# An attention and maxout feed-forward kernel: the four weight matrices arrive as fp32 through SyncE's queue and are narrowed to fp16 by GpSimd

## The chip, the cores and the metric

The kernel runs on one core of a Trainium2 chip. The metric is the device time of one execution in microseconds (us). The five engines of the core are called PE (TensorE, matrix products), DVE (VectorE), ACT (ScalarE), POOL (GpSimd) and SP (SyncE); SP does no arithmetic here and only issues transfers. Each engine carries out its own list of instructions strictly in order, and waits for others through semaphores.

## The reference

Attention for 4 batches of 8 heads, 768 positions, head size 64, scores scaled by 1/8. Heads 0, 2 and 6 see every earlier position; the other five see the first 4 positions and the last 64. Its result, 3072 tokens by 512, goes through a feed-forward with three weight matrices under a maximum:

```
full   = rel >= 0                                   # rel = query position - key position
stream = (rel >= 0) & ((key < 4) | (rel < 64))
scores = where(mask_of_head, q @ k.T / 8, -1e9)
a      = exp(scores - max) ; a = a / sum(a)
x      = (a @ v) as [4*768, 512]
h      = maximum(maximum(x @ w1, x @ w2), x @ w3)   # w1, w2, w3: 512 x 768
out    = h @ w_out                                  # w_out: 768 x 512
```

All inputs and the output are fp32; the kernel computes its products in fp16 with fp32 sums.

## The kernel before, in words

The work is cut into 8 half batches (batch b, half of 384 positions), and each half batch into two groups of four heads. A group is numbered t = 4b + 2 half + group, and its two pairs of heads i = 0, 1. Nothing plans the order at run time: the tuple `PROGRAM` (L46 to L97) is a list of steps, a loop at L677 emits them one after another, and every engine and every queue sees its own instructions in just that order. What matters of the list:

- `hl half hp n ss` (L299) issues, on SP, fp32 loads of q and k of n pairs of heads of batch 0; `cast half hp ee` (L208) narrows k and q of a pair with the two engines named; `turnp` (L220) transposes them on PE and copies them from PSUM. The staging of two-pair loads has two buffers, so `hl 1 2` waits for the casts of `hl 0 2`.
- `load b qd` (L248) loads k and q of later batches with POOL's queue, which narrows fp32 to fp16 on the way, into the staging tag `kq` (three buffers of 6 KB per partition); `turn` (L259) transposes them on DVE. `load_v b half` (L281) loads v with SP, three transfers of 256 KB; `v t i ab` (L498) narrows it with engine a (`va`) and multiplies the far copy `vf` with engine b.
- `s t u` (L518): score products on PE, exponential on ACT. `k t i u e` (L570): multiplies exponentials by a mask on engine e (p is POOL, d is DVE). `av t i` (L590): on PE, weights times v, which needs every mask of that t and i and both copies of v; then on DVE the division. `x` (L627) or a transfer transposes the result.
- `f 1 e` (L488): advances the feed-forward of the oldest finished half batch by one `yield`. One half batch is a generator (L417): 18 steps of four products each (L438) and 3 steps of output products (L474). For batch 0 the 18 steps go through all of `w0t`, then all of `w1t`, then all of `w2t`. Each output step has two yields, so every other output `f` emits nothing.
- `m` (L387) builds masks on DVE, `gate` (L668) makes SP wait for a group before it goes on.

The weights: `w wi` (L399) issues on POOL's queue a transfer that narrows fp32 to fp16 on the way and writes the final tile: `w0t` in two halves, `w1t`, `w2t` and `woutt` whole, 768 KB each as written. They are the only weight loads; all 8 half batches use the same tiles.

Around the change POOL's own list is: mask and v work, the two halves of `w0t`, cast of `1 2`, `v 0 1`, cast of `1 0`, `w1t`, mask `k 2 1 2`, `w2t`, `load 1 0`, `woutt`, `load 1 1`, masks `k 2 0 3`, `k 2 0 2`, `k 3 0 1`, then v work of groups 2 and 3. SP's list is: loads of q and k, `load_v 0 0` in two parts, `hl 1 2`, `load_v 0 1`, then from `av 2 0` on transposes and stores. PE's list is: `turnp 1 2`, `x 0 0`, `s 2 0 1`, `av 1 1`, `av 1 0`, `av 0 1`, `turnp 1 0`, scores, six steps on `w0t` between scores, `turnp 1 3`, six steps on `w1t`, `av 2 0`, two steps on `w2t` and so on.

Of the kernel before, what the change touches and what calls it, by code (L numbers as in the profile page):

```python
# [11 lines left out]
FP32 = mybir.dt.float32  # L12
# [31 lines left out]
FIRST = "hl 0 0 1, ir"  # L44

PROGRAM = (  # L46
    "idle 2, idle 8, cast 0 0 aa, hl 0 1 1 ss, hl 0 2 2 ss, read, hl 1 0 2 ss, cast 0 1 pp",
    "flags, cast 0 2 ap, em 1, turnp 0 1 a, far, em 0, turnp 0 0 aa, cast 0 3 da, em 2, em 3",
    "load_v 0 0 4 4, s 0 0 1, s 0 0 0, v 1 1 pp, cast 1 1 pa, turnp 0 3 dd, turnp 0 2 da",
    "w 0 2 0, load_v 0 0 0 4, v 0 0 dp, s 1 0 0, w 0 2 1, s 0 1 0 b, hl 1 2 2 ss, s 1 0 1",  # L50
    "cast 1 2 dp, v 1 0 dd, s 0 1 1, s 1 1 0 b, av 0 0, v 0 1 pp, turnp 1 1 a, s 1 1 1",
    "turnp 1 2 aa, x 0 0 a, s 2 0 1, cast 1 0 dp, load_v 0 1, cast 1 3 ad, av 1 1, s 2 1 1",
    "av 1 0, x 1 1 d, av 0 1, turnp 1 0 ad, s 2 2 1, x 1 0 d, s 3 0 0, m 0, w 1, x 0 1 d",
    "s 2 0 0, m 3, m 1, f 1 d, f 1 d, s 2 1 0, s 2 2 0, m 2, f 1 a, f 1 d, k 2 1 2 p, k 2 0 1 d",
    "w 2, f 1 d, s 2 3 1, load 1 0, w 3, k 3 0 0 d, s 3 1 0, f 1 a, s 2 3 0, load 1 1",
    "k 2 0 3 p, k 2 0 2 p, turnp 1 3 dd, k 3 0 1 p, k 2 1 1 d, k 2 1 3 d, f 1 d, f 1 d",
    "v 2 0 ad, f 1 a, f 1 a, v 3 1 pp, f 1 d, s 3 0 1, v 2 1 dp, s 3 1 1, f 1 a, v 3 0 ap",
    "av 2 0 D, f 1 d, f 1 d, s 3 2 0, turn 1 0 0 0, turn 1 0 0 1, f 1 a, turn 1 0 1 0, s 3 2 1",
    "s 3 3 0, k 3 0 2 p, k 3 1 2 p, turn 1 0 1 1, f 1 a, av 2 1 D, s 3 3 1, k 3 1 1 d",
    "k 3 0 3 p, k 3 1 3 p, f 1 a, k 3 1 0 d, load_v 1 0, gate, f 1 a, s 4 0, k 4 1 0 p",  # L60
    "v 4 0 pp, av 3 0, av 3 1, f 1 a, f 1 a, x 3 0 d, s 4 1, turn 1 1 0 1, x 3 1 a, f 1 d",
    "v 5 1 pp, turn 1 1 1 0, turn 1 1 1 1, turn 1 1 0 0, k 4 0 1 d, k 4 0 0 d, k 4 1 1 p, f 1 a",
    "f 1 a, f 1 d, load_v 1 1, f 1 a, f 1 a, f 1 a, v 4 1 pd, f 1 a, f 1 d, s 5 0, f 1 a, f 1 d",
    "av 4 0 D, k 5 0 0 d, f 1 d, s 5 1, k 5 0 1 p, load_v 2 0, f 1 a, f 1 a, load 2 0, f 1 a",
    "s 6 0, f 1 d, av 4 1 D, f 1 a, v 5 0 ap, f 1 a, s 6 1, f 1 a, av 5 0 D, f 1 d, f 1 d",
    "k 5 1 1 p, k 5 1 0 p, v 7 0 dp, s 6 2, k 6 1 2 p, f 1 a, av 5 1 D, turn 2 0 1 0, f 1 a",
    "v 6 0 ad, s 6 3, turn 2 0 0 1, x 5 1 d, f 1 a, turn 2 0 1 1, load 2 1, load 3 1",
    "load_v 2 1, v 6 1 ap, f 1 d, f 1 d, k 6 0 2 p, v 9 0 ap, k 6 1 3 p, f 1 a, f 1 a",
    "turn 2 0 0 0, s 7 0, f 1 a, f 1 d, f 1 d, turn 2 1 0 0, k 6 0 1 d, f 1 a, s 7 1, f 1 d",
    "f 1 a, f 1 a, k 6 1 1 p, k 7 1 1 d, f 1 d, s 7 2, f 1 a, f 1 a, k 6 0 3 p, k 7 1 2 d",  # L70
    "turn 2 1 1 0, load 3 0, av 6 0 D, s 7 3, f 1 d, v 7 1 pp, av 6 1 D, k 7 1 3 p, f 1 d",
    "turn 3 1 1 0, k 7 0 3 p, turn 2 1 0 1, s 8 0, k 7 0 1 p, turn 2 1 1 1, k 7 0 2 p, f 1 a",
    "f 1 d, load_v 3 0, k 8 0 0 p, av 7 1 D, s 8 1, f 1 a, f 1 a, s 9 0, v 8 0 ap, k 8 0 1 d",
    "f 1 a, f 1 d, av 7 0 D, v 13 1 pp, s 9 1, f 1 a, av 8 0 D, f 1 d, s 10 0, f 1 a, x 7 1 d",
    "f 1 a, v 10 0 dd, f 1 d, s 10 1, f 1 a, f 1 d, v 9 1 ad, f 1 a, f 1 d, f 1 a, s 10 2",
    "f 1 d, f 1 d, f 1 d, k 8 1 0 p, f 1 d, k 9 0 0 p, k 9 1 1 d, f 1 d, f 1 d, v 11 0 ad",
    "f 1 d, k 9 1 0 p, v 12 0 ad, k 9 0 1 p, k 8 1 1 d, av 9 0 D, v 8 1 ap, s 10 3, f 1 d",
    "f 1 a, av 8 1 D, turn 3 0 1 0, s 11 0, k 10 1 1 p, f 1 d, f 1 d, k 10 0 3 p, f 1 a",
    "av 9 1 D, v 13 0 ap, f 1 a, k 10 1 3 d, turn 3 0 1 1, x 9 1 a, k 10 0 1 p, s 11 1, f 1 a",
    "k 10 0 2 p, v 11 1 ap, av 10 0 D, f 1 d, s 11 2, k 11 0 2 p, turn 3 0 0 0, f 1 a",  # L80
    "turn 3 0 0 1, f 1 d, k 11 0 1 d, f 1 a, k 10 1 2 d, f 1 d, v 10 1 ap, f 1 a, turn 3 1 0 1",
    "f 1 a, f 1 a, s 12 0, av 10 1 D, f 1 a, f 1 d, k 12 1 0 p, s 12 1, f 1 d, f 1 a, f 1 a",
    "k 12 0 1 p, turn 3 1 0 0, s 11 3, v 12 1 ad, f 1 a, load_v 3 1, f 1 a, f 1 a, k 11 0 3 d",
    "k 11 1 3 p, f 1 d, f 1 d, k 11 1 1 p, turn 3 1 1 1, f 1 a, f 1 d, av 11 0 D, f 1 d",
    "k 11 1 2 d, f 1 a, k 12 0 0 p, k 12 1 1 d, f 1 a, s 13 0, av 12 0 D, f 1 d, av 11 1 D",
    "k 13 0 0 d, f 1 d, f 1 d, s 13 1, f 1 d, v 15 1 pp, f 1 d, k 13 0 1 p, x 11 1 d, f 1 d",
    "v 15 0 ad, av 12 1 D, k 13 1 1 d, av 13 0 D, s 15 0, f 1 a, f 1 d, f 1 d, f 1 a, f 1 d",
    "f 1 d, f 1 a, k 13 1 0 d, s 15 1, v 14 0 ap, f 1 d, f 1 a, f 1 d, f 1 d, s 14 0, f 1 a",
    "f 1 d, f 1 d, f 1 d, av 13 1 D, s 14 1, f 1 d, x 13 1 d, f 1 d, f 1 d, f 1 a, f 1 a",
    "s 14 2, f 1 a, k 14 1 2 p, v 14 1 ad, k 14 1 1 p, f 1 d, f 1 d, f 1 d, f 1 a, f 1 a",  # L90
    "k 15 0 1 p, s 14 3, f 1 d, k 14 0 3 p, f 1 a, f 1 d, s 15 2, f 1 a, f 1 d, f 1 d, f 1 d",
# [18 lines left out]
def kernel(  # L110
# [22 lines left out]
    NNB = DF // P  # L133
# [14 lines left out]
    stage = ctx.enter_context(tc.tile_pool(name="stage", bufs=3))  # L148
# [27 lines left out]
    cast = {}  # L176
# [142 lines left out]
    def idle_work(n):  # L319
# [13 lines left out]
        out=base, in_=base, compare_op=ALU.is_ge, fill=0.0,  # L333
# [4 lines left out]
        out=kept[:, 256:512], in_=base, compare_op=ALU.is_gt, fill=0.0,  # L338
# [5 lines left out]
        out=kept[:, 0:256], in0=kept[:, 256:512], in1=base, op=ALU.add  # L344
    )
    nc.vector.tensor_copy(out=kept[:, 256:512], in_=kept[:, 0:256])
    if n_sink > 0:
        nc.vector.tensor_scalar(
            out=kept[0:n_sink, 256:512], in0=base[0:n_sink, :],
# [11 lines left out]
    far = consts.tile([P, H, 4], FP16, name="far")  # L361
# [34 lines left out]
    w_t = [consts.tile([P, KS, DF], FP16, name=f"w{wi}t") for wi in range(3)]  # L396
    woutt = consts.tile([P, NNB, DMdl], FP16, name="woutt")

    def load_weight(wi, parts=1, part=None):  # L399
        n = DF // parts  # L400
        first = 0 if part is None else part * n
        for c in range(first, (DF if part is None else first + n) if wi < 3 else 0, n):
            nc.gpsimd.dma_start(
                out=w_t[wi][:, :, c : c + n],
                in_=(moe_w1, moe_w2, moe_w3)[wi][:, c : c + n].rearrange(
                    "(ks p) n -> p ks n", p=P
                ),
            )
        if wi == 3:
            nc.gpsimd.dma_start(  # L410
                out=woutt, in_=moe_w_out.rearrange("(ns p) m -> p ns m", p=P)
            )


    xT = {}

    def ffn(b, half):  # L417
# [33 lines left out]
        for n, (wi, ni) in enumerate(order):  # L451
# [4 lines left out]
            else:  # L456
                dst = acc[ni] if wi == 1 else hT[ni]
                nc.vector.tensor_tensor(  # L458
                    out=dst, in0=yy[:, 0:HALF], in1=acc[ni], op=ALU.max
                )  # L460
            yield
        for tb in range(HB):

            parts = 2 if last and tb == HB - 1 else 1
            n = DMdl // parts
            r0 = b * S + half * HALF + tb * P
            ot = fwork.tile([P, DMdl], FP32, tag="ot", name="ot")
            for c, op, eng in (
                (0, nc.scalar.copy if last else copy_out[0], nc.sync),
                (n, nc.vector.tensor_copy, nc.scalar),  # L470
            )[:parts]:
                yo = psum()
                for ns in range(NNB):
                    nc.tensor.matmul(  # L474
                        yo[:, 0:n],
                        hT[ns][:, tb * P : (tb + 1) * P],
                        woutt[:, ns, c : c + n],
                        start=(ns == 0), stop=(ns == NNB - 1),
                    )
                op(out=ot[:, c : c + n], in_=yo[:, 0:n])  # L480
                eng.dma_start(out=out[r0 : r0 + P, c : c + n], in_=ot[:, c : c + n])
            yield
            yield

    queue = []
# [141 lines left out]
    def turn_x(t, i, op=None):  # L627
# [18 lines left out]
    ops = {"d": dve, "a": act, "p": pool}  # L646
    engines = {"d": nc.vector, "p": nc.gpsimd}
# [4 lines left out]
        f=lambda n, e="a": fill(int(n), ops[e]),  # L652
# [4 lines left out]
        turn=lambda *a: turn(*map(int, a)),  # L657
# [14 lines left out]
        far=far_flags,  # L672
        em=lambda hp: head_masks(int(hp), True),
        m=lambda hp: head_masks(int(hp)),
        w=lambda wi, *p: load_weight(int(wi), *map(int, p)),
    )
    for line in PROGRAM:  # L677
        for item in line.split(", "):
# [37 lines left out]
```

## Time and profile before

| what | us |
|---|---|
| two runs | 199.69 and 200.13, median 199.91 |
| span of the profiled execution (no other time of it is recorded) | 199.9 |
| PE busy | 190.0 (95%) |
| DVE / ACT / POOL busy | 148.3 / 115.9 / 90.5 |
| PE busy in the first 45 us | 38.5 |
| PE busy from 45 to 180 us | 134.9 of 135 |
| narrowing transfers on POOL's queue | 7.87 MB as written, 21.9% of 16 DMA engines' span |
| SP's queue | 17.96 MB, 37.9% |

How to read it: the share of busy PE is an average. Up to 45 us PE is idle for 6.5 us in some ten pieces; afterwards it has no idle time to speak of until the last microseconds. What delays PE in the first 45 us is therefore seen at the end in full, as far as nothing takes it up. In the timelines below a line gives start, duration, engine, line of the kernel, operation, output and inputs, shapes and count, and in brackets the engine's idle time just before it and what ended that. DMA engines are sixteen, shared by all queues.

### The profile page before, as it was taken

The page shows a single profiled execution, that of the slowest core. Times are in us where ns is not written, and L with a number is a line of the kernel's source. Part 1 is how long each engine was busy: PE and PEld are TensorE (multiplying, and loading weights), DVE is VectorE, ACT ScalarE, POOL GpSimd, SP SyncE. Part 2 cuts the span into 40 slices and gives each one's busy share as a digit, 9 for nine tenths or more (in the row PEclk, how much of TensorE's full clock was granted, in tenths as well). Part 3 has the DMA queues.
Part 4 walks back from the last instruction along what each step waited for, and adds up shares of the span by engine and source line. Part 5 has one row for each costly group of instructions (what it writes and reads, how often), then busy time and mean ns, then how long its engine had stood idle before and what let it go on. Part 6 is the DMA issues. An engine that isn't in the chain of part 4 may idle for free.

```text
span 199.9 us, 5135 instructions
## 1 busy us (share of the span) xinstructions
PE 190.0 (95%) x2059; PEld 109.3 (55%) x2059; DVE 148.3 (74%) x311; ACT 115.9 (58%) x171; POOL 90.5 (45%) x118
## 2 busy tenths in 40 slices
PE   7688898999999999999999999999999999999993
PEld 2345444565556455666456645574656455765552
DVE  3638965998976789896469998996978288767750
ACT  4489983765658798687776756634366565100011
POOL 3429187583276598490697245652010197000000
PEclk9889999999999999999999999999999999999999
DMA  5999999995979989988521232703500120124004
GB/s 143 312 245 230 196 195 212 208 169 76 283 173 211 162 169 208 218 218 176 147 76 23 43 124 74 159 20 73 167 5 20 53 108 0 23 59 157 3 0 157
DMA packets 48429, 26.48 MB, mean 132 GB/s; under 512 B 36758, under 2 KB 43926, under 8 KB 48406
## 3 DMA queue, kind: packets, MB, share of 16 engines
q1 hardware_dynamic: 43366, 17.96, 37.9%
q0 software_dynamic: 4624, 7.87, 21.9%
q8 instruction: 16, 0.26, 0.6%
q10 hardware_dynamic: 416, 0.33, 0.5%
q14 instruction: 7, 0.06, 0.1%
HBM read 25.17 MB, written 6.29 MB: 157 GB/s over the span
## 4 chain that ended last, share of the span: by engine, by line
PE 75%; DMA 11%; DVE 4%; SPq 3%; issue 2%; ACT 2%; POOL 0%; DVEq 0%
PE yy L438 39%; PE yy L474 14%; PE st L553 9%; PE oacc L602 9%; DMA vs<-in_v_dram 7%; PE yst L438 3%; DMA qs<-in_q_dram 2%; DVE KQ L267 2%; SPq L187 2%; ACT pt L564 1%; DMA xT<-x 1%; PE yst L474 1%; DVE acc L458 1%; DVE hT L458 1%; SPq L621 1%
## 5 line engine op out<-in xcount | busy, mean ns | idle before, releaser
L564 ACT ACTIVATE pt<-st 128x1024 f16<-128x1024 f32 (+3 forms) x98 | 83.3, 905 | 33.0 <-PE st L553 31.0
L586 POOL TENSOR_TENSOR pt<-pt,mk 128x512 f16<-128x512 f16 (+1 forms) x54 | 57.3, 1088 | 38.4 <-ACT pt L564 20.1
L438 PE MATMUL yy<-xT,w1t 128*128 128x384 f16 x180 | 35.8, 327 | 1.2 <-DVE pt L586 1.2
L438 PE MATMUL yy<-xT,w2t 128*128 128x384 f16 x180 | 36.1, 326 | 0.0
L438 PE MATMUL yy<-xT,w0t 128*128 128x384 f16 x180 | 35.8, 327 | 0.3
L458 DVE TENSOR_TENSOR acc<-yy,acc 128x384 f16<-128x384 f32 x45 | 24.8, 557 | 10.7 <-PE yy L438 8.6
L474 PE MATMUL yy<-woutt,hT 128*128 128x512 f16 (+1 forms) x138 | 31.6, 375 | 0.0
L553 PE MATMUL st<-KQ 32*128 32x384 f16 (+5 forms) x560 | 29.4, 281 | 1.4 <-ACT pt L564 0.8
L458 DVE TENSOR_TENSOR hT<-yy,acc 128x384 f16<-128x384 f32 x45 | 24.8, 556 | 4.5 <-PE yy L438 2.3
L602 PEld LDWEIGHTS <-pt 128*128 128x128 f16 x672 | 24.4, 97 | 4.8 <-DVE va L504 0.7
L267 DVE STREAM_TRANSPOSE KQ<-kq 128x384 f32<-128x384 f32 x24 | 25.5, 1132 | 0.6 <-DMA kq<-in_q_dram 0.6
L602 PE MATMUL oacc<-va,pt 128*128 128x65 f16 x352 | 24.9, 193 | 0.5 <-DVE va L504 0.5
L438 PEld LDWEIGHTS <-w1t 128*128 128x128 f16 x192 | 17.5, 98 | 14.1 <-issue 1.6
L438 PEld LDWEIGHTS <-w0t 128*128 128x128 f16 x192 | 17.8, 98 | 13.4 <-issue 0.8
L438 PEld LDWEIGHTS <-w2t 128*128 128x128 f16 x192 | 17.3, 98 | 11.9 <-issue 1.4
L553 PEld LDWEIGHTS <-KQ 32*128 32x128 f16 (+1 forms) x560 | 12.2, 93 | 18.8 <-issue 11.8
L474 PEld LDWEIGHTS <-hT 128*128 128x128 f16 x150 | 13.8, 98 | 14.7 <-issue 0.8
L602 PE MATMUL oacc<-vf,pt 128*128 128x65 f16 x320 | 21.1, 193 | 0.0
L455 ACT CAST acc<-yy 128x384 f16<-128x384 f32 x25 | 12.0, 481 | 13.9 <-PE yy L438 13.5
L612 DVE TENSOR_TENSOR x<-oacc,rc 128x384 f16<-128x384 f32 x32 | 17.8, 557 | 1.1
L480 DVE COPY ot<-yy 128x512 f32<-128x512 f32 (+1 forms) x15 | 10.1, 675 | 9.2 <-PE yy L474 9.2
L506 POOL TENSOR_TENSOR vf<-va,far 128x384 f16<-128x384 f16 x10 | 8.6, 867 | 17.3 <-ACT va L504 12.9
(72 smaller groups left out, 143.4 us busy)
## 6 DMA issues: line engine op xcount, KB each, us to landing
out_dram<-ot SPq DMA_DIRECT2D x23, 256.0 KB, 2.1
vs<-in_v_dram SPq DMA_DIRECT2D x21, 256.0 KB, 5.6
kq<-in_k_dram POOLq DMA_DIRECT2D x6, 384.0 KB, 7.9
kq<-in_q_dram POOLq DMA_DIRECT2D x6, 384.0 KB, 10.0
ks<-in_k_dram SPq DMA_DIRECT2D x8, 192.0 KB, 3.6
qs<-in_q_dram SPq DMA_DIRECT2D x7, 192.0 KB, 4.8
vs<-in_v_dram SPq DMA_DIRECT2D x6, 128.0 KB, 4.8
w0t<-in_moe_w_dram POOLq DMA_DIRECT2D x2, 384.0 KB, 9.4
```

Source lines behind the costliest of these rows:

```text
L267: nc.vector.transpose(out=dst.rearrange("c (p j) -> c j p", j=n)[:, j0:j1], in_=src.rearrange("c (j i) -> c j i", i=R),)
L438: nc.tensor.matmul(yy[:, 0:HALF], w_t[wi][:, ks, ni * P : (ni + 1) * P], xT[b, half][ks].rearrange("p a t -> p (a t)"), start=(ks == 0), s ...
L455: copy_out[0](out=acc[ni], in_=yy[:, 0:HALF])
L458: nc.vector.tensor_tensor(out=dst, in0=yy[:, 0:HALF], in1=acc[ni], op=ALU.max)
L474: nc.tensor.matmul(yo[:, 0:n], hT[ns][:, tb * P : (tb + 1) * P], woutt[:, ns, c : c + n], start=(ns == 0), stop=(ns == NNB - 1),)
L480: op(out=ot[:, c : c + n], in_=yo[:, 0:n])
L506: vf_engine.tensor_tensor(out=vf[j][:, hs, k0:k1, 0:D], in0=vs[:, hs, 0:1] if half == 0 else va[j][:, hs, k0:k1, 0:D], in1=far[:, hs, k0:k ...
L553: nc.tensor.matmul(sts[g // m][:, g % m, c0 : c0 + n * P], KQ[rows, 0, ki * P : (ki + 1) * P], KQ[rows, 1, t0 : t0 + n * P], start=(c0 == ...
L564: nc.scalar.activation(out=pts[t, i][:, u, h0 : h0 + m, 0:w], in_=st[:, :, 0:w], func=AF.Exp, scale=sc,)
L586: engine.tensor_tensor(out=x, in0=x, in1=m, op=ALU.mult)
L602: nc.tensor.matmul(o[:, qi, hl, 0 : D + 1], pt[:, u, hl, c : c + P], vv[:, 2 * hp + hl, ki, 0 : D + 1], start=(idx == 0), stop=(idx == len ...
L612: nc.vector.tensor_tensor(out=x, in0=o[:, :, :, 0:D], in1=rc.unsqueeze(3).to_broadcast([P, HB, 2, D]), op=ALU.mult,)
```

## The change

The weights no longer narrow in the transfer. Each matrix comes in two halves of 768 KB fp32 through SP's queue into a staging tile of 128 x 1536 fp32 from the tag `kq`, the same three buffers that `load` uses. A new step `c wi part pp` narrows a half into the weight tile with two POOL copies of 128 x 768 each. In `PROGRAM` the eight `w` steps and the eight `c` steps stand at places of their own, among other steps whose order is otherwise the same. The second yield of an output step goes, and with it the 24 `f` steps that emitted nothing; what the remaining `f` steps emit, and between which other steps, is the same as before.

```
-    "w 0 2 0, load_v 0 0 0 4, v 0 0 dp, s 1 0 0, w 0 2 1, s 0 1 0 b, hl 1 2 2 ss, s 1 0 1",
-    "cast 1 2 dp, v 1 0 dd, s 0 1 1, s 1 1 0 b, av 0 0, v 0 1 pp, turnp 1 1 a, s 1 1 1",
-    "turnp 1 2 aa, x 0 0 a, s 2 0 1, cast 1 0 dp, load_v 0 1, cast 1 3 ad, av 1 1, s 2 1 1",
-    "av 1 0, x 1 1 d, av 0 1, turnp 1 0 ad, s 2 2 1, x 1 0 d, s 3 0 0, m 0, w 1, x 0 1 d",
-    "s 2 0 0, m 3, m 1, f 1 d, f 1 d, s 2 1 0, s 2 2 0, m 2, f 1 a, f 1 d, k 2 1 2 p, k 2 0 1 d",
-    "w 2, f 1 d, s 2 3 1, load 1 0, w 3, k 3 0 0 d, s 3 1 0, f 1 a, s 2 3 0, load 1 1",
-    "k 2 0 3 p, k 2 0 2 p, turnp 1 3 dd, k 3 0 1 p, k 2 1 1 d, k 2 1 3 d, f 1 d, f 1 d",
+    "load_v 0 0 0 4, w 0 0, v 0 0 dp, s 1 0 0, s 0 1 0 b, w 0 1, hl 1 2 2 ss, s 1 0 1",
+    "cast 1 2 dp, v 1 0 dd, s 0 1 1, s 1 1 0 b, av 0 0, v 0 1 pp, turnp 1 1 a, s 1 1 1, c 0 0 pp",
+    "turnp 1 2 aa, x 0 0 a, w 1 0, s 2 0 1, cast 1 0 dp, w 1 1, load_v 0 1, cast 1 3 ad, c 0 1 pp",
+    "av 1 1, s 2 1 1, av 1 0, c 1 0 pp, x 1 1 d, av 0 1, turnp 1 0 ad, s 2 2 1, w 2 0, c 1 1 pp",
+    "w 2 1, x 1 0 d, s 3 0 0, m 0, x 0 1 d, s 2 0 0, m 3, m 1, f 1 d, f 1 d, s 2 1 0, s 2 2 0",
+    "m 2, c 2 0 pp, w 3 0, f 1 a, f 1 d, k 2 1 2 p, k 2 0 1 d, f 1 d, s 2 3 1, c 2 1 pp, w 3 1",
+    "load 1 0, k 3 0 0 d, s 3 1 0, c 3 0 pp, f 1 a, s 2 3 0, load 1 1, k 2 0 3 p, c 3 1 pp",
+    "k 2 0 2 p, turnp 1 3 dd, k 3 0 1 p, k 2 1 1 d, k 2 1 3 d, f 1 d, f 1 d, v 2 0 ad, f 1 a",
...
-    def load_weight(wi, parts=1, part=None):
...
+    raw = {}
+
+    def load_weight(wi, part):
+        st = stage.tile([P, 1536], FP32, tag="kq", name="wst")
+        if wi < 3:
+            n = DF // 2
+            nc.sync.dma_start(
+                out=st.rearrange("p (ks n) -> p ks n", n=n),
+                in_=(moe_w1, moe_w2, moe_w3)[wi][:, part * n : part * n + n].rearrange(
                     "(ks p) n -> p ks n", p=P
                 ),
             )
+        else:
+            n = NNB // 2 * P
+            nc.sync.dma_start(
+                out=st.rearrange("p (ns m) -> p ns m", m=DMdl),
+                in_=moe_w_out[part * n : part * n + n].rearrange("(ns p) m -> p ns m", p=P),
+            )
+        raw[wi, part] = st
+
+    def cast_weight(wi, part, engines):
+        st = raw.pop((wi, part))
+        if wi < 3:
+            n = DF // 2
+            src = st.rearrange("p (ks n) -> p ks n", n=n)
+            dst = w_t[wi][:, :, part * n : part * n + n]
+        else:
+            n = NNB // 2
+            src = st.rearrange("p (ns m) -> p ns m", m=DMdl)
+            dst = woutt[:, part * n : part * n + n]
+        m = dst.shape[1]
+        for i, op in enumerate(engines):
+            x = slice(i * m // len(engines), (i + 1) * m // len(engines))
+            op(out=dst[:, x], in_=src[:, x])
...
             yield
-            yield
```

## The prediction

> **What bounds the kernel now.** I read the slices of the span first, for the stages; then who waited for whom up to 50 us; then the timelines of PE and POOL between 14 and 37 us, where the change lies. The slices (each 5.0 us):
>
> ```profile
> PE   7688898999999999999999999999999999999993
> POOL 3429187583276598490697245652010197000000
> DMA  5999999995979989988521232703500120124004
> ```
>
> PE is full from slice 8 on (134.9 of the 135 us from 45 to 180). Only before that does it wait, and at the same time the DMA engines are full. So the weights lie where a delay costs. Two waits, of PE's loads and of PE, show the only place where a weight is late:
>
> ```profile
> PEld L438 <- DMA w1t<-in_moe_w_dram: 1.4, 1, 1.4
> PE yy L438 <- DVE pt L586: 1.2, 1, 1.2
> ```
>
> They are one stall, before the first product with `w1t` at 30.97; `w1t` was issued at 18.77 and took 12.2 to land, which ends at 30.97, so it is the transfer. At most this 1.2 is to be had from weights that come sooner. PE's line of that place, and the two that I count from below:
>
> ```profile
> 17.39 0.34 PE L231 MATMUL tr<-ident,kn 128*128 128x128 f16 x3
> 30.97 3.42 PE L438 MATMUL yy<-xT,w1t 128*128 128x384 f16 x20 [1.22 <-DVE pt L586]
> 35.68 0.22 PE L602 MATMUL oacc<-vf,pt 128*128 128x65 f16 x2
> ```
>
> The last is `av 2 0`. It needs the masks `k 2 0 3` and `k 2 0 2`, which are POOL's, the first two of the three here:
>
> ```profile
> 18.77 0.81 POOL L403 DMA_DIRECT2D w1t<-in_moe_w_dram  x1
> 24.24 1.14 POOL L586 TENSOR_TENSOR pt<-pt,mk 128x512 f16<-128x512 f16 x1 [4.67 <-DVE mk L389]
> 25.34 0.81 POOL L403 DMA_DIRECT2D w2t<-in_moe_w_dram  x1
> 31.00 3.06 POOL L586 TENSOR_TENSOR pt<-pt,mk 128x512 f16<-128x512 f16 x3 [1.86 <-ACT pt L564]
> 34.10 0.50 POOL L504 CAST va<-vs 128x384 f16<-128x384 f32 x1
> ```
>
> So `k 2 0 2` ends at 33.05 (two of three masks of 1.02), 2.6 before PE wants it. That is all the room POOL has.
>
> **The change, part by part.** The empty steps: what the other steps emit keeps its order, so 0 from both sides. The five issues on POOL that go free 4.2 of POOL (0.93, 0.82, 0.81, 0.81, 0.86 in its timeline).
>
> *Price of a cast.* No 128x768 cast is in the trace. POOL's 128x384 cast takes 0.50; a memset takes 0.31 at 256 and 0.21 at 128 columns, 0.10 per 128, so 0.80 is the low end; two casts of 384 are 1.0, and with the slope of POOL's masks (1.17 at 512, 0.68 at 256) it is 1.07, the high end. I take 0.85, near the memset's slope since a cast reads one input like it rather than two like a mask. A half is two casts, 1.7 (1.6 to 2.15); eight halves are 13.6. Between 18.77 and 33.05 POOL idles 4.7 + 1.9 = 6.5, and with the 4.2 it has 10.7 of room there. So even without waits POOL's masks slip by 2.9, which uses the 2.6.
>
> *Price of a transfer.* By the trace's packets a read of 768 bytes takes 36 ns on one of 16 engines and a store of 2048 bytes 86, so 1536 bytes come to 66 ns. A half has 512 of them (768 KB): 512 x 66 / 16 = 2.1. The cast transfers take 78 ns (768 bytes written), 135 (1536) and 98 (1024): 5.2 + 8.8 + 4.7 = 18.8 for all weights against 16.8 now. The 2.0 gained by the DMA engines I count at nothing, because order, not volume, decides below. From the last packet to the waiter's start it is 0.8 (first half of v, 14.46 to 15.29) to 2.4 (`w1t`, 28.55 to 30.97); SP's other part of v has 1.7; I take 1.1, nearer to the two of SP's own queue. From issue to first packet 1.1 (0.81 to 1.92).
>
> *What is moved on SP's queue.* `w 0 0` and `w 0 1` now stand ahead of `hl 1 2`. The packets of one queue follow one another: v ends at 14.46, `hl 1 2` runs from about 14 to 16.96. Two halves push it by 4.2, and its third quarter, the q half that POOL casts, ends at 20.1 and not 15.87. Landed: 21.2. Behind the waiting POOL cast stand all of POOL's later work; behind DVE's half of that cast (now about 20) stand `v 1 0` and the division of `av 0 0`; PE waits at `turnp 1 2` until 21.8, against 17.39, +4.4. By itself that is the size of the loss up to here.
>
> *The new wait on SP.* Three buffers: `w 1 1` must wait until POOL has cast `w 0 0`, and `load_v 0 1` and everything later on SP stands behind it. POOL: cast of `1 2` to 21.7, `v 0 1` (0.51 + 0.40) to 22.6, `c 0 0` to 24.3. Then `w 1 1`: first packet 25.4, 2.1, to 27.5; `load_v 0 1`, 3072 packets of 256 bytes, 512 of them in 0.64 while undisturbed, so 3.8, to 31.3; `w 2 0` (its buffer is free by 26.5) to 33.4, landed 34.5. `load_v 0 1` itself lands near 32.4; before, its last packets ended at 33.6, slowed by the cast transfers beside them: no loss there, and the group that reads it is later anyway.
>
> *POOL from there to `av 2 0`.* POOL has done `c 0 1`, `c 1 0` and `c 1 1` and waits for `w 2 0`. Then, in order: `c 2 0` 1.7, `k 2 1 2` 1.1, `c 2 1` 1.7, `load 1 0` 1.1 (0.55 + 0.56), `c 3 0` 1.7, `load 1 1` 1.1, `k 2 0 3` 1.1, `c 3 1` 1.7, `k 2 0 2` 1.1: 12.3. On SP each of the eight issues takes some 0.5 (as a 192 KB load), while SP has nothing else, and its last new wait (`w 3 1` for `c 2 0`, 36.2) is over long before the transposes of `av 2 0`. The transfers of `w 2 1` (35.5), `w 3 0` (37.6) and `w 3 1` (39.7) land before their casts. So `k 2 0 2` ends at 34.5 + 12.3 = 46.8. PE, 4.4 late and without the 1.2 for `w1t`, is at `av 2 0` at 38.9 and stands until 46.8 instead of starting at 35.7: **+11.1**, in which the 4.4 is contained. ACT and DVE then have nothing open, and POOL's next masks (51 to 55.5) follow a group that is 11.1 later as well, as before; nothing gives time back, since PE waits nowhere after 45. `load 1 0` lands near 46, its transposes begin at 38.8 + 11.1: covered.
>
> *PE after a stand of 8 us.* The granted clock after the short idleness at 6 to 8 us:
>
> ```profile
> 6.00:8.00 2.00, 0.38 (x7) 0.38 (x8) 1.15 (x6) 0.45 (x1) 0.56 (x1) 1.00 1.06 334
> 8.00:10.00 2.00, 2.00 (x18) 1.13 (x15) 1.76 (x5) 2.00 (x6) 1.26 (x3) 0.54 1.10 331
> 10.00:12.00 2.00, 2.00 (x21) 1.40 (x19) 0.97 (x3) 2.00 (x3) 0.08 (x1) 0.61 1.25 248
> ```
>
> (Per stage: busy time of PE, PE's loads, DVE, ACT and POOL, then the clock.) It fell to 0.54 and 0.61: 2 x 0.46 + 2 x 0.39 = 1.7 of full clock lost. After the new stand PE has dense work, so it pays this, **+1.7**; the bounds are 0 and twice that. The first new stand (17.4 to 21.8) pays too, but its loss lies inside the second.
>
> **Sum**: 199.9 (the span; the median of the runs is 199.91, so nothing is added) + 11.1 + 1.7 = **212.7**.
>
> **Rivals.** *A, order on the queue does not matter*: packets of several loads interleave or land sooner, and POOL waits no more after `c 0 1`. Then POOL's 10.6 after `c 2 0` follow directly on `c 0 1` (26.5), `c 1 0`, `c 1 1`, `c 2 0`: 26.5 + 5.1 + 10.6 = 42.2, +6.5, with the clock 208.1, without it 206.4. If `hl 1 2` is not pushed either, 4.2 less: 202.2 to 203.9. For it: DMA shares above 1.0, so packets overlap. Against: the loads of the first 17 us appear strictly one after another.
>
> *B, POOL and DVE hold each other up.* DVE's masks of 128x512 take 0.41 beside an idle POOL and up to 1.06 when a POOL mask runs, so one can wait for a whole instruction of the other. If each of the ten casts in the chain is held once by 0.5, it is +5: 217.7. The Trainium skill, "SBUF — State Buffer", section "Who interferes with whom", speaks against the change in the same sense: GpSimd shares one pair of ports with VectorE, and whichever starts first keeps it for the whole instruction. The trace agrees by the 1.06. Against it here: from 39 to 47 DVE has nothing to do.
>
> *C, not slower.* The place is again `av 2 0`: if POOL finishes `k 2 0 2` before 35.7, the stall goes and 1.2 is won: 198.7. That needs POOL to pack 13.6 into 10.7 + 2.6 and never to wait, so casts of 0.8 or less and `hl 1 2` not pushed; every us of waiting beyond that is lost. The empty steps can't help. The low price is possible, the absence of waits hardly.
>
> **How the numbers follow.** Forecast 0.72, A 0.14 (0.04 of it without the push of `hl 1 2`), B 0.08, C 0.06. The forecast's own terms: casts (five halves lie in the sum) -0.5 to +2.2, landings (two) -0.6 to +2.6, clock -1.7 to +1.7; all at one end they give 209.9 and 219.2, which rarely meet, so I let it go to 218. With A's lower time: 206 to 218, which leaves out C, A without the push, and the far tail of B. 2% is 4.0, about what a measurement of this kernel can tell from no change: slower than 203.9 is 0.90; within it 0.06, A's 0.04 and 0.02 of C; faster 0.04, the rest of C.
>
> **What would show it.** In the profile after: POOL's cast of `qn` near 21 behind a wait for its transfer; PE's wait at L231 of 4 us; copies of 128x768 at 0.85; `c 2 0` starting near 34.5 after a wait for its staging tile; PE standing some 8 us until the last mask near 46.8, then a granted clock of about half for 3 to 4 us; from there the same length to the end. I am wrong if `hl 1 2` lands before 18, if a cast is far from 0.85, or if POOL runs its list without waits.

## The result

The changed kernel takes 216.85 us (216.45 and 217.26) against 199.91 before: slower by a ratio of 1.085 (95% interval 1.079 to 1.090). In a later comparison, beside the experiments, it took 216.0 against 200.83, 1.075 (1.069 to 1.082). Single executions of all these kernels spread by 1 to 2%, so below I also compare places in the profiles, which spread less; the profiled execution of e8 was a disturbed one, so only who waited for whom is read from it.

The profiled execution after has a span of 214.8, and its own time is 216.45: 1.65 lie around the span. The slices of the span after (5.4 us each):

```profile
PE   7781799509999999999989999999999999999994
POOL 4330863996837548949319745464201059100000
DMA  5999399894088699999574022370330012024004
```

PE has a hole in the fourth slice (16.1 to 21.5 us) and a larger one in the eighth and ninth (37.6 to 48.3), in which POOL is full; from the tenth slice on PE is as full as before. The waits of PE up to 60 us that bear on it:

```profile
PE oacc L619 <- POOL pt L603: 7.1, 1, 7.1
PE tr L230 <- DVE kn L211: 4.0, 1, 4.0
PE tr L230 <- POOL qn L211: 3.2, 2, 1.9
PE yy L456 <- DVE acc L476: 0.9, 1, 0.9
```

The long wait for `w1t` is gone, and two stands are new: 4.0 and 1.9 at `turnp 1 2`, 7.1 at `av 2 0`. POOL's timeline after shows how the second comes about (start, duration, what, and in brackets its idle time before and what ended it):

```profile
22.29 0.50 POOL L211 CAST qn<-qs 128x384 f16<-128x384 f32 x1 [7.27 <-DMA qs<-in_q_dram]
...
23.55 1.59 POOL L431 CAST w0t<-wst 128x768 f16<-128x768 f32 x2
...
35.56 1.60 POOL L431 CAST w2t<-wst 128x768 f16<-128x768 f32 x2 [3.82 <-DMA wst<-in_moe_w_dram]
37.12 1.32 POOL L603 TENSOR_TENSOR pt<-pt,mk 128x512 f16<-128x512 f16 x1
38.39 1.78 POOL L431 CAST w2t<-wst 128x768 f16<-128x768 f32 x2
40.49 0.72 POOL L250 DMA_DIRECT2D kq<-in_k_dram  x1 [0.32 <-POOL w2t L431]
...
41.74 1.61 POOL L431 CAST woutt<-wst 128x512 f16<-128x512 f32 x2
...
45.80 1.59 POOL L431 CAST woutt<-wst 128x512 f16<-128x512 f32 x2
47.36 1.76 POOL L603 TENSOR_TENSOR pt<-pt,mk 128x512 f16<-128x512 f16 x2
```

POOL waits 7.3 for the q that is queued behind two weight halves, then 3.8 for the first half of `w2t`; from there it works with no more than two pauses of 0.3, and the mask `k 2 0 2`, the first of the last line, ends at 48.5. Between the two waits lies SP's: of the 9.79 in which it issues `w 1 0` and `w 1 1`, 8.0 are a wait for POOL's cast of the first half of `w0t`, and v and `w 2 0` stand behind it.

```profile
15.75 9.79 SPq L404 DMA_DIRECT2D wst<-in_moe_w_dram  x2
25.58 3.99 SPq L286 DMA_DIRECT2D vs<-in_v_dram  x3
29.67 1.57 SPq L404 DMA_DIRECT2D wst<-in_moe_w_dram  x2
```

PE in the same execution, at `turnp 1 2` and at `av 2 0`:

```profile
22.85 0.50 PE L230 MATMUL tr<-ident,qn 128*128 128x128 f16 x3 [1.93 <-POOL qn L211]
41.19 0.23 PE L619 MATMUL oacc<-vf,pt 128*128 128x65 f16 x2
48.56 0.29 PE L619 MATMUL oacc<-va,pt 128*128 128x65 f16 x2 [7.14 <-POOL pt L603]
```

Product by product (both kernels have the same 2059 on PE, in the same order), PE is behind the kernel before by this much:

| where (time in the kernel before) | behind, us |
|---|---|
| `turnp 1 2`, q part (17.6) | 5.2 |
| first product with `w0t` (23.6) | 6.1 |
| first product with `w1t` (31.0) | 4.6 |
| fifth product step with `w1t` (33.6) | 5.7 |
| `av 2 0` after its mask (35.7) | 12.8 |
| 38.0, clock full again | 14.3 |
| first product of the second half batch (50.4) | 14.1 |
| 97.6, a transposed x that lands late | 14.9 |
| last products (196) | 14.9 |

### The profile page after: what moved, and what is told of

Same layout as the page of the kernel before. It is cut to its first block, busy times and chain, and to the rows that moved or that the text cites. A ratio compares the mean times of both kernels' runs of the same rounds, so it can differ in the third digit from the quotient of the medians.

```text
span 214.8 us, 5157 instructions
## 1 busy us (share of the span) xinstructions
PE 192.7 (90%) x2059; PEld 111.5 (52%) x2059; DVE 153.7 (72%) x311; ACT 116.2 (54%) x171; POOL 99.2 (46%) x129
## 4 chain that ended last, share of the span: by engine, by line
PE 75%; DMA 10%; POOL 8%; issue 3%; SPq 3%; DVE 0%; POOLq 0%
PE yy L456 39%; PE yy L492 14%; PE oacc L619 10%; PE st L570 9%; DMA qs<-in_q_dram 6%; PE yst L456 3%; DMA wst<-in_moe_w_dram 2%; POOL pt L603 2%; POOL w2t L431 2%; POOL woutt L431 1%; SPq L286 1%; DMA vs<-in_v_dram 1%; DMA xT<-x 1%; SPq L186 1%; PE yst L492 1%
## 5 line engine op out<-in xcount | busy, mean ns | idle before, releaser
L456 PE MATMUL yy<-xT,w2t 128*128 128x384 f16 x180 | 36.9, 332 | 0.0
L456 PE MATMUL yy<-xT,w0t 128*128 128x384 f16 x180 | 35.7, 326 | 0.9 <-DMA xT<-x 0.9
L619 PE MATMUL oacc<-va,pt 128*128 128x65 f16 x352 | 26.4, 199 | 7.2 <-POOL pt L603 7.1
L619 PEld LDWEIGHTS <-pt 128*128 128x128 f16 x672 | 25.9, 100 | 11.8 <-POOL pt L603 7.3
L570 PE MATMUL st<-KQ 32*128 32x384 f16 (+5 forms) x560 | 29.9, 283 | 1.0 <-DVE KQ L238 0.7
L619 PE MATMUL oacc<-vf,pt 128*128 128x65 f16 x320 | 22.1, 197 | 0.0
L473 ACT CAST acc<-yy 128x384 f16<-128x384 f32 x25 | 12.0, 480 | 14.7 <-PE yy L456 14.3
L603 DVE TENSOR_TENSOR pt<-pt,mk 128x512 f16<-128x512 f16 (+1 forms) x32 | 16.9, 550 | 0.6 <-ACT pt L581 0.6
```

The source lines that it names most:

```text
L456: nc.tensor.matmul(yy[:, 0:HALF], w_t[wi][:, ks, ni * P : (ni + 1) * P], xT[b, half][ks].rearrange("p a t -> p (a t)"), start=(ks == 0), s ...
L473: copy_out[0](out=acc[ni], in_=yy[:, 0:HALF])
L570: nc.tensor.matmul(sts[g // m][:, g % m, c0 : c0 + n * P], KQ[rows, 0, ki * P : (ki + 1) * P], KQ[rows, 1, t0 : t0 + n * P], start=(c0 == ...
L603: engine.tensor_tensor(out=x, in0=x, in1=m, op=ALU.mult)
L619: nc.tensor.matmul(o[:, qi, hl, 0 : D + 1], pt[:, u, hl, c : c + P], vv[:, 2 * hp + hl, ki, 0 : D + 1], start=(idx == 0), stop=(idx == len ...
```

## The experiments

Two places are used for comparison: the start of the part of `av 2 0` that needs the masks, and PE's first product of the second half batch with `w0t` ("second half batch"). They are at 48.56 and 64.58 in the changed kernel (48.57 and 64.71 in its repetition), at 35.74 and 50.44 in the kernel before.

| kernel | time, ratio to before | `av 2 0` | second half batch |
|---|---|---|---|
| e1: loads of `hl 1 2` first | 214.84, 1.072 (1.064 to 1.080) | 46.35 | 62.14 |
| e2: v ahead of the waiting half | 215.24, 1.074 (1.069 to 1.080) | 47.23 | 63.88 |
| e3: w_out cast late | 216.50, 1.082 (1.075 to 1.089) | 43.95 | 65.62 |
| e4: PE kept busy | 216.87, 1.079 (1.070 to 1.089) | 48.75 | 63.30 |
| e5: casts on ACT and POOL | 214.43, 1.069 (1.064 to 1.073) | 47.04 | 63.51 |
| e6: short casts | 213.78, 1.066 (1.061 to 1.070) | 47.30 | 63.99 |
| e11: short loads | 210.86, 1.049 (1.043 to 1.055) | 43.48 | 59.85 |
| e10: short loads and casts | 207.68, 1.030 (1.022 to 1.037) | 39.97 | 56.13 |
| e8: half of the weights staged | 203.18, 1.013 (1.009 to 1.017) | | |
| e9: the same, in another order | 209.79, 1.044 (1.039 to 1.049) | 41.88 | 58.05 |
| e7: kernel before, `w1t` in halves | 0.998 (0.994 to 1.002) | 34.35 | 48.88 |
| e12: the change again | 216.00, 1.075 (1.069 to 1.082) | 48.57 | 64.71 |

The intervals of e1 to e6 overlap that of the change in e12, so their times alone do not tell them from it; what is said of them rests on the places, from one profile each. A place carries some 0.3: the start of POOL's cast of q, which e2 to e6 leave alone, lies between 22.00 and 22.56.

**e1, the loads of q and k first.**

```
-    "load_v 0 0 0 4, w 0 0, v 0 0 dp, s 1 0 0, s 0 1 0 b, w 0 1, hl 1 2 2 ss, s 1 0 1",
+    "load_v 0 0 0 4, v 0 0 dp, s 1 0 0, s 0 1 0 b, hl 1 2 2 ss, w 0 0, w 0 1, s 1 0 1",
```

> The two halves of w1 (w 0 0 and w 0 1) stand behind hl 1 2 on SP's queue again, all else as in the changed kernel. Theory 1 (the chain of the prediction: the push delays POOL, POOL's cast of w 0 0 holds SP, w 2 0 lands late, the masks follow): POOL casts qn at about 18 and not 22.3, PE no longer stands 4 us at turnp 1 2, w 2 0 is landed at about 32.4 and not 35.6, k 2 0 2 ends at about 45.4 and not 48.5; 216.9 - 3.1 = 213.7. Rival 1 (POOL has simply too much work, the order on SP's queue does not matter): within 1 of 216.9. Rival 2 (the push is a loss of its own, every us of the first stand is seen at the end): 216.9 - 4.8 - 1.4 of clock = 210.7.

POOL cast qn at 17.74, and PE stood 1.0 at `turnp 1 2` instead of 5.9 (and 1.8 at `turnp 1 0`); it came to `av 2 0` only 1.9 behind the kernel before instead of 5.5. But there it stood 8.6 instead of 7.1, since `w 2 0` was cast at 33.04, only 2.5 sooner. So the 3.6 us less were worth 2.2 at `av 2 0` (2.4 at the second half batch), and these come through POOL's chain. The first stand is not a loss of its own, and the order on the queue does matter.

**e2, v ahead of the half that waits for a buffer.**

```
-... cast 1 0 dp, w 1 1, load_v 0 1, cast 1 3 ad ...
+... cast 1 0 dp, load_v 0 1, w 1 1, cast 1 3 ad ...
```

> w 1 1, the first half that must wait for a staging buffer, stands behind load_v 0 1 on SP instead of ahead of it, all else as in the changed kernel. Theory 1 (SP stands behind POOL's cast of w 0 0 and the DMA engines run dry meanwhile): load_v 0 1 fills the gap of the DMA engines from 24.3 to 26.2, w 2 0 lands at about 31.7 and not 35.6, k 2 0 2 ends at about 44.7; 216.9 - 3.8 = 213.1. Rival 1 (POOL has too much work whatever the transfers do): within 1 of 216.9. Rival 2 (the DMA engines' volume decides, not the gap): w 2 0 lands where it did, since the same bytes stand ahead of it; 216.9.

A miss in size: 1.3 sooner at `av 2 0`, 0.7 at the second half batch. v's packets did fill the gap (22.6 to 27.4). But `w 1 1` then ran from 26.8 to 30.6 and `w 2 0` from 30.0 to 32.4. POOL was at the cast of the later `w 1 1` until 32.9, waited another 1.2 for `w 2 0` and began on it at 34.16, 1.8 after its last packet (0.7 in the changed kernel). The gap is worth about a third of what I gave it.

**e3, the casts of w_out behind the masks.**

```
-    "load 1 0, k 3 0 0 d, s 3 1 0, c 3 0 pp, f 1 a, s 2 3 0, load 1 1, k 2 0 3 p, c 3 1 pp",
+    "load 1 0, k 3 0 0 d, s 3 1 0, f 1 a, s 2 3 0, k 2 0 3 p",
-... v 3 0 ap, av 2 0 D ...
+... v 3 0 ap, c 3 0 pp, load 1 1, av 2 0 D ...
-... k 3 0 3 p, k 3 1 3 p, f 1 a ...
+... k 3 0 3 p, k 3 1 3 p, c 3 1 pp, f 1 a ...
```

> The casts of both halves of w_out and load 1 1 move behind the masks k 2 0 3 and k 2 0 2 in POOL's list: c 3 0 and load 1 1 behind the v work of groups 2 and 3, c 3 1 behind the last mask of group 3. Theory 1 (PE stands at av 2 0 for POOL's list, one us for one us): two pairs of casts, 3.2, load 1 1, 1.1, and its 0.3 of waiting go from ahead of k 2 0 2, which ends at about 43.9 and not 48.5; PE starts av 2 0 4.6 sooner; up to 1 comes back at av 3 0, where the masks now stand behind c 3 0: 212.3 to 213.3. Rival 1 (w2 or its transfer holds PE there, the masks being late beside it): within 1 of 216.9.

The first part came out to 0.05 us: `av 2 0` at 43.95, 4.6 sooner. But all of it came back. PE's lines of this kernel with a wait from there on:

```profile
43.95 0.23 PE L619 MATMUL oacc<-va,pt 128*128 128x65 f16 x2 [2.67 <-POOL pt L603]
54.00 0.20 PE L619 MATMUL oacc<-va,pt 128*128 128x65 f16 x1 [1.79 <-POOL pt L603]
57.91 0.23 PE L619 MATMUL oacc<-va,pt 128*128 128x65 f16 x1 [2.36 <-DVE pt L603]
```

1.8 were lost at `av 3 0`, whose masks now stand behind `c 3 0` (I had allowed 1). The 2.4 at `av 3 1` I had not thought of: they are a mask on DVE, `k 3 1 1`. DVE's line, and POOL's at the same time:

```profile
52.24 5.61 DVE L603 TENSOR_TENSOR pt<-pt,mk 128x256 f16<-128x256 f16 x1
```

```profile
50.55 4.50 POOL L603 TENSOR_TENSOR pt<-pt,mk 128x512 f16<-128x512 f16 x4
54.99 1.58 POOL L431 CAST woutt<-wst 128x512 f16<-128x512 f32 x2
56.55 1.83 POOL L603 TENSOR_TENSOR pt<-pt,mk 128x512 f16<-128x512 f16 x2
```

The same mask takes 0.28 before:

```profile
44.92 0.28 DVE L586 TENSOR_TENSOR pt<-pt,mk 128x256 f16<-128x256 f16 x1
```

It took 5.61 while POOL worked without a pause, and came through late in POOL's last line, just after its first mask. That POOL's work is what held it fits all the profiles here: of DVE's masks and far copies, 322 overlap no POOL instruction, and none of them is more than 0.06 longer than the shortest of its shape; all 111 that are longer by over 0.35 overlap one. After these stands the clock was at half from 56.4 to 63.3, and the second half batch came 1.0 later than in the changed kernel. So PE follows POOL's list one for one at `av 2 0`, and w2 and its transfer don't hold it there; but a fuller POOL list afterwards holds DVE.

**e4, PE kept busy in the stand.**

```
-... v 3 0 ap, av 2 0 D ...
+... v 3 0 ap, idle 30, av 2 0 D ...
```

> Thirty products of zeros (128x512, some 0.22 each, 6.5 in all) are put on PE ahead of av 2 0, into the 7.1 us in which it stands; all else as in the changed kernel. Theory 1 (of the loss some 1.5 is the clock: after the stand PE works at half clock from 48.6 to 51.8): av 2 0 starts at 48.5 as before, the granted clock stays 1.00 from 45 on, and the time is 216.9 - 1.5 = 215.4. Rival 1 (PE is not what limits after the stand, the half clock is hidden): 216.9. Rival 2 (the products run into the end of the stand): over 216.9.

The stages 45 to 55 us of the changed kernel, then of this one (busy us of PE, PE's loads, DVE, ACT, POOL; then granted clock, DMA share, GB/s):

```profile
45.00:50.00 5.00, 1.44 (x27) 1.45 (x28) 0.00 (x0) 0.00 (x0) 4.92 (x7) 0.50 1.03 203
50.00:55.00 5.00, 4.96 (x40) 2.45 (x38) 3.89 (x7) 2.19 (x3) 3.19 (x5) 0.82 0.13 26
```

```profile
45.00:50.00 5.00, 4.62 (x49) 2.60 (x48) 0.16 (x1) 0.00 (x0) 4.92 (x7) 1.00 1.08 210
50.00:55.00 5.00, 4.96 (x59) 2.82 (x58) 4.92 (x9) 2.86 (x4) 4.67 (x6) 1.00 0.15 31
```

The clock stayed at 1.00, `av 2 0` started 0.2 later, and the second half batch 1.3 sooner: so 1.5 was the clock, as expected. The time did not show it and came out as rival 1 has it (216.87): in the profiled execution PE later waited 2.2 for a transposed x that landed late, where the changed kernel waited 0.9 and e12 hardly at all. That wait differs from run to run and can cover a gain of this size; whether it did in the other executions is not on record.

**e5, casts on two engines.** Every `c wi part pp` became `c wi part ap`.

> Of the two casts of each half the first goes to ACT and the second stays on POOL, at the same places of the list; all else as in the changed kernel. Theory 1 (POOL's work ahead of the masks is the loss, and moving work off POOL is what helps): four casts of 0.8 and one in c 0 0 go from POOL's chain, k 2 0 2 ends at about 44.7 and not 48.5, the second half batch's first product with w0t starts at about 60.8 and not 64.6: 216.9 - 3.8 = 213.1. Rival 1 (ACT now stands in order at c 2 0 until w 2 0 has landed near 35, ahead of its copies of acc and its exponentials): PE stands sooner, the masks wait for ACT's exponentials, and the time is 216 or more.

The mask `k 2 0 2` ended 2.5 sooner, at 45.96 (theory 1 wanted 44.7), but `av 2 0` started only 1.5 sooner. ACT stood 1.1 and 1.8 at two casts whose halves had not landed, so its copy of v came late, and DVE's far copy of v after it. PE's wait ended with DVE's `acc`, which stands right behind that copy. DVE's line, POOL's beside it, and PE's:

```profile
43.29 3.15 DVE L523 TENSOR_TENSOR vf<-va,far 128x384 f16<-128x384 f16 x1 [3.45 <-ACT va L521]
```

```profile
42.70 1.17 POOL L603 TENSOR_TENSOR pt<-pt,mk 128x512 f16<-128x512 f16 x1
43.81 1.04 POOL L431 CAST woutt<-wst 128x1024 f16<-128x1024 f32 x1
44.80 2.16 POOL L603 TENSOR_TENSOR pt<-pt,mk 128x512 f16<-128x512 f16 x2
```

```profile
46.97 0.27 PE L619 MATMUL oacc<-vf,pt 128*128 128x65 f16 x2 [3.79 <-DVE acc L476]
```

This operation takes 0.56 before (at 34.60, between two instructions of POOL); here it took 3.15, while POOL went from one instruction to the next, as in e3. The prediction's rival B decided here, on DVE's side and not on POOL's, where I had put it.

**e6, short casts.** Two thirds of w1, w2 and w3 are left out: only the first 128 columns of each half are narrowed, and the products read them three times.

```
-            src = st.rearrange("p (ks n) -> p ks n", n=n)
-            dst = w_t[wi][:, :, part * n : part * n + n]
+            src = st.rearrange("p (ks n) -> p ks n", n=n)[:, :, 0:P]
+            dst = w_t[wi][:, :, part * n : part * n + P]
-                    w_t[wi][:, ks, ni * P : (ni + 1) * P],
+                    w_t[wi][:, ks, ni // 3 * 3 * P : (ni // 3 * 3 + 1) * P],
```

> The casts of w1, w2 and w3 narrow only the first 128 of each half's 384 columns, and the products with w1, w2, w3 all read those 128 columns, so two thirds of the three weight matrices are left out of the result; all transfers, all products and the casts of w_out stay. A cast of 128x256 should take about 0.38 in place of 0.80. Theory 1 (POOL's chain as in the prediction: it starts anew when w 2 0 lands, so only c 0 0, c 2 0 and c 2 1 count): k 2 0 2 ends 3 x 0.84 = 2.5 sooner, at about 46.0; 214.4. Rival 1 (the sum of POOL's work counts, whatever it waits for): six halves, 5.0: 211.9. Rival 2 (the transfers alone hold POOL, the casts lie in its waits): 216 to 217.

Half of theory 1's 2.5: 1.3 at `av 2 0`, 0.6 at the second half batch. The casts fell to 0.37 each, but POOL turned the time into waits (4.7 ahead of `c 2 0` and not 3.8, then 0.2 and 0.8 for halves that it had found landed). The duration of the casts alone does not explain the stand, so I formed theory 2: two limits close together.

**e11 and e10, short loads with whole casts, and with short casts.** Of w1, w2 and w3 only the first 128 columns of each half are transferred, the others are left out of the result; e11 reads them three times in casts of full length, e10 adds this to e6.

```
-                out=st.rearrange("p (ks n) -> p ks n", n=n),
-                in_=(moe_w1, moe_w2, moe_w3)[wi][:, part * n : part * n + n].rearrange(
+                out=st.rearrange("p (ks n) -> p ks n", n=n)[:, :, 0:P],
+                in_=(moe_w1, moe_w2, moe_w3)[wi][:, part * n : part * n + P].rearrange(
...
+            src = src.unsqueeze(2).to_broadcast([P, KS, 3, P])     # e11 alone
```

> Transfers of w1, w2 and w3 bring only the first 128 of each half's 384 columns, but the casts still write 768 columns each, reading those 128 three times; the other columns are left out of the result. Theory 2 (two limits close together): the transfers no longer hold POOL, its list does: k 2 0 2 ends at about 43.4 and not 48.5, the second half batch starts some 5 us sooner than in the changed kernel, 211.5. Rival 1 (POOL's casts alone are the loss): 216 to 217. Rival 2 (the transfers alone are): as with both short, some 2.5 lower than theory 2.

> As the kernel with short casts, and the transfers of the halves of w1, w2 and w3 also bring only their first 128 of 384 columns, so two thirds of these three matrices are neither loaded nor narrowed and are left out of the result; w_out is whole. Theory 2, formed after the first runs (two limits lie close together, the transfers on SP's queue and POOL's list, so that lifting one alone shows the other): POOL waits for hardly any half, k 2 0 2 ends at about 40.8 against 47.9 with short casts alone, the second half batch's first product with w0t starts some 7 us sooner, and the time is near 207 to 209. Rival (POOL's list alone, or the volume of work whatever its order): not below 212.

Against the 64.6 of the changed kernel the second half batch starts 0.6 sooner with short casts, 4.7 with short loads, 8.5 with both: more than the sum of the two, as theory 2 wants. POOL's lines of e11 show the second limit: after a wait of 2.7 instead of 3.8 the list is full, and the stand stays 6.4. (The wait is put down to DVE here; the half's last packet ended at 29.04, 1.25 before the cast.)

```profile
30.29 1.78 POOL L434 CAST w2t<-wst 128x768 f16<-128x768 f32 x2 [2.71 <-DVE acc L476]
32.03 1.15 POOL L606 TENSOR_TENSOR pt<-pt,mk 128x512 f16<-128x512 f16 x1
33.13 1.98 POOL L434 CAST w2t<-wst 128x768 f16<-128x768 f32 x2
```

`k 2 0 2` ended at 43.4 (43.4 expected) and 39.9 (40.8); the times are 210.9 (211.5) and 207.7 (207 to 209). In either order short loads give more (4.7 alone, 7.9 after short casts) than short casts (0.6 and 3.7). So the larger part of what these two take away lies in the transfers on SP's queue, the smaller in POOL's casts; 5.7 remain with both.

**e8 and e9, half of the weights staged.** `w3` and `w_out` go back to narrowing transfers on POOL's queue (a step `wq`), `w1` and `w2` stay staged, behind `hl 1 2`.

```
+    "cast 1 2 dp, ... s 1 1 1, c 0 0 pp",                              # e8
+    "turnp 1 2 aa, x 0 0 a, w 1 0, s 2 0 1, cast 1 0 dp, w 1 1, load_v 0 1, cast 1 3 ad, c 0 1 pp, wq 2",
...
+    "load 1 0, wq 3, k 3 0 0 d, s 3 1 0, f 1 a, s 2 3 0, load 1 1, k 2 0 3 p",
+    "cast 1 2 dp, ... s 1 1 1",                                         # e9
+    "turnp 1 2 aa, x 0 0 a, w 1 0, s 2 0 1, cast 1 0 dp, load_v 0 1, cast 1 3 ad, c 0 0 pp, wq 2, c 0 1 pp",
+    "w 1 1, av 1 1, s 2 1 1, ..."
```

> Only w1 and w2 (the halves of w0t and w1t) come through SP and are cast by POOL, behind hl 1 2; w3 and w_out come narrowed by the transfer on POOL's queue as in the kernel before, w3 right behind c 0 1. POOL then has 4 x 1.6 = 6.4 of casts, less 2.6 of issues, and needs not wait for w 2 0. Theory 1 (POOL has about 2.6 + 6.5 of room before av 2 0, and the loss is what exceeds it): POOL is through k 2 0 2 at about 36 to 37, PE's stand at av 2 0 is under 2, and the time is 201 to 203. Rival 1 (the staging and SP's waits are the loss, however few the halves): the stand stays over 5, 210 or more. Rival 2 (the weight that is late in the kernel before was the only thing to win): 198.7.

203.18 is 1.3% above the kernel before (200.73 beside it), where theory 1 wanted 201 to 203: with POOL's work halved and no wait for `w 2 0`, most of the loss is gone. PE no longer stands at `av 2 0`; it stands 2.7 at `turnp 1 0`, whose cast is queued behind `c 0 0`, which itself waited 2.9 for its half. e8 also puts `hl 1 2` first, as e1 does, so it does not tell these parts from each other.

> As the kernel with half of the weights staged (w1 and w2 through SP, w3 and w_out narrowed by the transfer), but POOL casts the first half of w1 behind the cast of pair 1 0 instead of ahead of it, and w 1 1, which waits for that cast, stands behind load_v 0 1. Theory 1 (what is left of the loss there, 2.4 us, is PE's stand of 2.7 at turnp 1 0, because POOL waits for w 0 0 ahead of the cast that turnp 1 0 needs): the stand goes, the stall of 1.2 at the first product with w1t does not come back, and the time is 203.1 - 2.7 = 200.4, within 0.5% of the kernel before. Rival 1 (staging costs that much wherever the casts stand, through the ports that POOL and DVE share): 203. Rival 2 (w2t, narrowed by the transfer beside the halves, is late): over 202.

A clear miss. That stand went, and PE was at the first product with `w1t` 0.9 ahead of the kernel before. But `w 1 1` was now issued at 24.88, behind v, whose packets ran until 31.07 beside the narrowing transfer of `w3` (24.29 to 30.36), and its own ran from 29.6 to 33.4; POOL's line:

```profile
33.85 1.60 POOL L442 CAST w1t<-wst 128x768 f16<-128x768 f32 x2 [7.08 <-DMA wst<-in_moe_w_dram]
```

POOL waited 7.1 for it, with `w1t` (2.6 of PE) and the masks (2.3) behind. POOL late for a half that is late on SP's queue: the same mechanism as in the change, made by two moved steps. Rival 2's time came out (over 202), but not its cause: PE waited for `w1t`, not for `w2t`.

**e7, the kernel before with `w1t` in two halves.**

```
-... m 0, w 1, x 0 1 d
+... m 0, w 1 2 0, w 1 2 1, x 0 1 d
```

> The kernel before, with w1t loaded in two halves instead of whole, at the same place, still narrowed by the transfer on POOL's queue. One more issue on POOL, 0.8. Theory 1 (the one stall that weights cause before is the 1.2 us ahead of the first product with w1t, and its first half can land some 2 us sooner): PE starts on w1t at about 29.8 and not 31.0, POOL's masks have room for the 0.8, and the time falls by 1.2: 199.9 - 1.2 = 198.7, ratio 0.994. Rival 1 (the halves' packets, 768 bytes, take 78 ns against 135 for 1536, so the second half comes 0.7 later and holds the fourth product): no change. Rival 2 (what PE gains is lost at the next wait, w2t): no change.

In the profile the stall is gone: PE is 0.2 behind at the first product with `w0t`, 1.2 ahead at the first with `w1t`, 1.6 ahead at the second half batch, and 0.7 ahead at the end, after a wait of 1.0 for a transposed x. The times don't separate it from the kernel before: ratio 0.998 (0.994 to 1.002). So it is at best a gain of 0.6%, and none of the versions is shown to beat the kernel before.

**e12, the change again.**

> The changed kernel once more, beside these runs and with the kernel before on the same chip, since single executions of both spread by 1%. Every theory expects 216 to 217.5 here; it is to tell how far the comparisons above may be trusted.

216.0, at the lower edge. The two places agree with the first profile to 0.15 us; the late x, worth 0.8 there, is missing here.

## Why the prediction was right

Direction, place and mechanism held: POOL's masks for `av 2 0` are late because the cast of q, then the first half of `w2t`, are late on SP's queue, and POOL has no room for the casts. Step by step:

| step | predicted | measured |
|---|---|---|
| packet of 1536 bytes | 66 ns | 65 to 69 |
| cast of 128x768, half of a pair | 0.85 | 0.80 |
| q of `hl 1 2`: last packet, then POOL's cast | 20.1, 21.2 | 20.04, 22.29 |
| `w 2 0` cast from | 34.5 | 35.56 |
| from there to the end of `k 2 0 2` | 12.3 | 12.9 |
| PE behind at `av 2 0` | 11.1 | 12.8 |
| clock after the stand | 1.7 | 1.5 |
| later | 0 | 0.8 |
| span | 212.7 | 214.8 |

**The terms that were mis-sized.** Landing: I took 1.1 from the last packet to the waiting cast; it was 2.25 for q. The value lies within the bounds that I had from the trace (0.8 to 2.4), and I took the wrong end. It is one us of the 1.7 that are missing at `av 2 0`. That it reaches `w 2 0` at this size is luck: on the way the packets of `w 1 1` took 3.06 and not 2.1 (26.22 to 29.28), which was made up by v's packets, which began before these had ended (0.5), and by a landing of only 0.74 for `w 2 0` (0.4). The other 0.6 are POOL's chain: two waits of 0.3 ahead of its own transfers of `load`, for the cast that frees their buffer, which I had not counted, and masks of up to 1.32 against 1.1, less 0.3 that the shorter casts gave back. "Nothing gives time back, since PE waits nowhere after 45" held for the losses, but one wait of 0.9 came new, at a transposed x.

Two readings were wrong without entering the sum. POOL's three masks at 31.00 before take 1.32, 1.15 and 0.66, not 1.02 each, so `k 2 0 2` ends at 33.4 and POOL's room is 2.3, not 2.6. And the high end of a cast does not come out of the rows named for it: 0.50 and 1.5 times the 0.49 between the two masks are 1.24, not 1.07.

**The step that was wrong** is the sum's first: "the median of the runs is 199.91, so nothing is added". The time of an execution is 1.65 more than its span (216.45 against 214.8). The profiled execution before, with 199.9 of span, would have taken 201.6, so it was one of the slower ones: beside the experiments the kernel before had spans from 197.7 to 199.1 in most executions. By spans the loss is 14.9, by medians 16.9. Of the 2.0 between them 1.6 is this choice of the execution to start from (199.91 less 1.65 is a span of 198.3), and 0.4 that the profiled execution after was the faster of its two. So the two profiles account for 14.9 of the loss; in the later comparison the medians differ by 15.2.

The measured time lies in the stated range, 1.15 below its upper end. The 2.1 in the terms are what the range was made for; the 2.0 of the first step are not, and that it held both is luck.

**The rivals.** A (order does not matter) fell with e1 and the wait of 7.3 in POOL's line. Its idea that POOL never waits fell with the 3.8; and e11 and e10 show that even short loads leave 9.4 and 5.7. B (POOL and DVE hold each other up) is seen but hidden in the stand: two DVE masks of 128x512 took 0.75 before and 2.20 after,

```profile
30.56 0.75 DVE L586 TENSOR_TENSOR pt<-pt,mk 128x512 f16<-128x512 f16 x2
```

```profile
36.53 2.20 DVE L603 TENSOR_TENSOR pt<-pt,mk 128x512 f16<-128x512 f16 x2
```

which cost PE the 0.9 at `w1t`, 10 us ahead of the end of a stand that covers it. (DVE, which was to have nothing to do from 39 on, worked until 44.0.) The casts themselves grew little (0.83 to 1.02), so the 5 us that I gave B on POOL's side are not there. The rule that the Trainium skill, "SBUF — State Buffer", section "Who interferes with whom", gives (the later one waits for the whole instruction of the other) agrees with these 2.20 in kind; in e3 and e5 the wait outlasted several instructions (5.61 against 0.28, 3.15 against 0.56). C asked for POOL to pack its list without waits; it waited 7.3, 1.3 and 3.8. Of C's gain, the 1.2 at `w1t`, PE did get 1.5 back between the first products with `w0t` and with `w1t`, and e7's profile shows that it can be had without staging.

The empty steps: PE's order of products is the same in both kernels, and its distance stays 14.14 from 43 to 80 us of the kernel before, so I see no trace of them. They weren't tried alone.

**What stays open.** Staging with more buffers, so that SP never waits for POOL, wasn't tried. How much of the transfers' part is the push, the wait for buffers and the volume is settled only roughly: 2.4 for the push (e1), 0.7 for the gap (e2), 4.7 for short loads with whole casts (e11).

## What to carry to other kernels

A transfer that narrows on its way holds no engine but its issuer for 0.8 us; the same data brought wide and cast by an engine costs that engine 1.6 a half, and it stands in order with everything else that engine owes. Before moving work to an engine with 45% busy time, count its room ahead of the next thing that the bound engine needs from it. Here that was 6.5 us of idle time, 4.2 of issues that went and 2.3 to spare, 13.0 in all, for 12.8 of casts: enough only if POOL never waited, and it waited 12.4 in three places. So look what is queued behind each transfer and each wait that is moved. And a POOL list packed without gaps can hold DVE's two-input operations for several us (5.6 here), so where a move frees time at one place, look for the next place at which POOL, or DVE behind it, is late.

## What was not expected of the hardware

- DVE products with two SBUF inputs took 5.61 instead of 0.28 (128x256, e3) and 3.15 instead of 0.56 (128x384, e5) while POOL went from one instruction to the next without a pause. DVE was held not over one instruction of POOL's but over several, so a POOL list without gaps can shut such an operation out. That it does not always (most such operations that overlap POOL grow by less than 0.35) stays unexplained.
- From a transfer's last packet to the start of the waiting instruction there were 0.7 to 2.3 us on the same queue; the last packets of one half come up to 1.3 after nine tenths of them (`w 2 1` in e2: 34.36 and 35.65).
- SP's three issues of `load_v 0 1`, which take 3.0 before, took 8.5 in e2 and 9.3 in e9, without a buffer to wait for, while the transfers ahead of them were still draining.
- After the stand of 7.1 the granted clock was 0.50 for 6.8 us (44.96 to 51.79), of which 3.2 fell on work.
